# Attention and a gated MLP in one kernel: an opening of 108 tiny matmuls, queries loaded without their zeros, and a new order

## The chip, the cores and the metric

The kernel runs on one core of a Trainium2 chip. The metric is the device time of one execution in microseconds, the median of several runs; lower is better.

## The reference

`q`, `k`, `v` have 8 batches, 8 heads, 576 positions and 64 columns; `x` then has 4608 tokens of 512.

```python
scores = 1/sqrt(64) * q @ k.T
rel = pos[:, None] - pos[None, :]
mask_local = (rel >= 0) & (rel < 32)                       # heads 0 to 3
mask_strided = (rel >= 0) & (pos[None, :] % 32 == pos[:, None] % 32)   # heads 4 to 7
attn = softmax(where(mask, scores, -1e9))                  # the sum has 1e-9 added
x = (attn @ v), heads side by side                         # (4608, 512)
xn = x / sqrt(mean(x * x, -1) + 1e-6) * rms_g
g = xn @ w_gate                                            # 512 -> 1536
out = (g * sigmoid(g) * (xn @ w_val)) @ w_out              # 1536 -> 512
```

## The kernel before

**Attention.** A unit is one batch and one pair of heads; there are 32, numbered 0 to 31. For each unit TensorE computes the scores (`unit_s`; S0, S1, ... below) only where the mask can let something through: 576 queries of two heads lie on 128 partitions, and for each there are 9 groups of 64 keys. VectorE takes the maximum of each group of 64 (L726, L730), ScalarE the exponentials, in nine activations that also give the sums (L743), VectorE multiplies by the reciprocal (L766, L767, L775) and transposes 32x32 blocks (L776), and TensorE multiplies with the values (`unit_o`; P0, P1, ... below). Unit 3 is the one unit in `HALFQ`: there VectorE subtracts the maximum (L736), one activation takes the exponential of all 576 columns (L762), and VectorE sums (L763).

For units 0 to 7 (`EIGHT`) the queries of the two heads come from DRAM as one block of 128 x 1152 with zeros in it: in the 64 partitions of one head the columns of the other head are zero, so that one matmul with a stationary operand of 128 x 64 serves both heads. The mask is added on TensorE by two bf16 matmuls with the identity ahead of the scores (L706), and `scores` (L718) then issues 18 f32 matmuls; the trace shows 36, since the compiler splits each in two. The values take 40, shown as 80 (L810). Units 0 to 3 (`NPRO`) are the prologue: their inputs lie in slots of their own.

**MLP.** The tokens go in 9 chunks of 512. Chunk 0 is done plainly, while the weights are still being converted: `gemm1` gives gate (key g) and value (key v) for each of 12 blocks of 128 columns of d_ff, "d_ff unit 0 to 11", and `slot_o` adds to the output in the banks a0 to a3, which ScalarE empties at the end (L1164). Chunks 1 to 8 go in pairs with a scheme of seven products for eight (L1250 for gate and value, L1403 for the output). Every f32 operand is split into a high and a low part, and a product takes three matmuls. The weights are split and combined once, by VectorE and ScalarE, and spilled to DRAM (`gvd`, `od`, `wd`), from where the later chunks load them. The sum of squares of chunk 0 goes through a matmul with ones (L888).

**Order.** Nothing in the code's order of statements fixes what runs when. Each operation is handed to `op` with an estimated cost; `Plan.order` and `Plan.forward` then go through all operations by list scheduling with these costs and the table `DUE` (one priority for each operation) and write the program of each engine in that order. `PLACE` says which slot of SBUF each group of tiles uses. Where the plan has TensorE idle for more than `FILLA` ns in the first 50 us, `fill` puts matmuls there that multiply zeros (`still`, L616) into a bank that is written afresh later; they compute nothing. The program of each engine is in order, and an instruction waits for semaphores of the others. PSUM banks are named g, v, a0 to a3 and pair (two banks); in the rows that order the instructions a0 to a3 are a_85 to a_88, and bl_N is a tile in a slot.

**The opening.** The first operation on TensorE comes some time after the start, and `fill` puts ten wide fillers (512 columns) ahead of it. Pool sets `still` to zero (L612):

```python
    op("Pool", 100, 0, lambda: nc.gpsimd.memset(still, 0.0), writes=["still"])
    def fill(n, pad):
        for _ in range(n):
            nc.tensor.matmul(out=pad[:, CH - FILLN:CH], lhsT=still[:, 0:P], rhs=still[:, 0:FILLN], ...
```

The order on TensorE is then S0, S1, S2, a filler, P0, S3, P1, a filler, P2, three fillers with three gate matmuls of d_ff unit 0 among them, P3, two fillers, S4, three value matmuls, the sum of squares, nine gate matmuls, three value matmuls, S5, and on.

## Time and profile before

| | |
|---|---|
| time, median of 3 runs | 909.78 us (908.98 to 911.97) |
| profiled execution | 910.43 us, of which the span 908.7 |
| TensorE clock granted, mean | 0.994 of full |
| busy: TensorE matmul, weight load | 886.8 us (98%), 716.8 us |
| busy: VectorE, ScalarE, GpSimd | 713.1 us (78%), 544.7 us (60%), 1.2 us |
| DMA | 234.25 MB, 258 GB/s in the mean |

The busy shares are means over the whole span; the first 60 us, where the attention of the first units, the conversion of the weights and chunk 0 run side by side, are not like the rest. The rows below are of the profiled execution, in us from the start of its span.

### The profile page before, as it was taken

The numbers are of one execution on the slowest core, as the hardware profiler recorded it, in microseconds if no ns is written. First come the engines' busy times: TensorE is split into PE (matmuls) and PEld (weight loads), VectorE is DVE, ScalarE is ACT, GpSimd is POOL, SyncE is SP. The second block draws the span as 40 slices with busy tenths as digits, with TensorE's granted clock in tenths as the row PEclk, the third lists the DMA queues.
The fourth block names the chain that finished last, engine by engine and source line by source line (L and its number), as shares of the span: only waits on it lengthen the run. The fifth ranks groups of instructions, "written<-read, shape, count | busy, mean of one in ns | idle before, by whom it ended". The sixth has DMA issues, their size and how long they took to land.

```text
span 908.7 us, 20785 instructions
## 1 busy us (share of the span) xinstructions
PE 886.8 (98%) x8289; PEld 716.8 (79%) x8292; DVE 713.1 (78%) x1203; ACT 544.7 (60%) x1179; POOL 1.2 (0%) x12
## 2 busy tenths in 40 slices
PE   6899999899999999999999999999999999999998
PEld 4677778678878888888887888888888888888886
DVE  4889989999998999667679998554799973338982
ACT  6799978677777784455537673444559533333440
POOL 0000000000000000000000000000000000000000
PEclk9899999999999999999999999999999999999999
DMA  9799999989987857876747559955365796742741
GB/s 357 269 400 413 413 414 366 403 330 403 359 286 272 284 175 268 292 269 195 231 145 243 169 172 334 341 161 179 105 196 174 230 369 214 210 148 70 248 136 69
DMA packets 104512, 234.25 MB, mean 258 GB/s; under 512 B 11616, under 2 KB 13920, under 8 KB 102112
## 3 DMA queue, kind: packets, MB, share of 16 engines
q1 hardware_dynamic: 103696, 232.34, 73.2%
q8 instruction: 65, 1.06, 0.5%
q10 hardware_dynamic: 720, 0.59, 0.2%
q14 instruction: 31, 0.25, 0.1%
HBM read 180.98 MB, written 51.90 MB: 256 GB/s over the span
## 4 chain that ended last, share of the span: by engine, by line
PE 82%; DMA 10%; DVE 3%; ACT 3%; issue 1%; SPq 0%; DVEq 0%
PE a L1250 22%; PE g L1250 14%; PE v L1250 14%; PE a L1403 11%; PE g L1403 7%; PE v L1403 7%; DMA wd<-bl 3%; DMA gvd<-bl 2%; DMA od<-bl 2%; PE pair L712 2%; PE pair L797 1%; DMA bl<-in_kT_dram 1%; PE a L797 1%; ACT pp L743 1%; DMA xk<-in_kT_dram 1%
## 5 line engine op out<-in xcount | busy, mean ns | idle before, releaser
L1250 PE MATMUL a<-bl,bl 128*128 128x512 f32 x856 | 216.7, 394 | 3.9 <-ACT bl L1164 3.0
L1250 PEld LDWEIGHTS a<-bl,bl 128*128 128x128 f32 x856 | 158.2, 188 | 39.2 <-ACT bl L1164 3.8
L594 ACT CAST bl<-bl 128x512 fp32r<-128x512 f32 (+1 forms) x209 | 126.7, 638 | 80.3 <-DVE bl L1206 37.6
L602 DVE TENSOR_TENSOR bl<-bl,bl 128x512 fp32r<-128x512 f32 x244 | 159.9, 687 | 8.2 <-ACT bl L594 2.1
L1250 PE MATMUL v<-bl,bl 128*128 128x512 f32 x571 | 146.0, 390 | 0.0
L1250 PE MATMUL g<-bl,bl 128*128 128x512 f32 x567 | 145.1, 390 | 0.0
L1206 DVE TENSOR_TENSOR bl<-bl,bl 128x512 f32<-128x512 f32 x169 | 113.7, 687 | 35.1 <-ACT bl L1267 33.5
L1250 PEld LDWEIGHTS v<-bl,bl 128*128 128x128 f32 x571 | 106.8, 188 | 23.1 <-DVE bl L1288 0.6
L1250 PEld LDWEIGHTS g<-bl,bl 128*128 128x128 f32 x567 | 106.0, 188 | 23.1 <-DVE bl L1288 0.7
L1262 DVE TENSOR_TENSOR a<-a,bl 128x512 f32<-128x512 f32 x96 | 66.6, 697 | 72.6 <-PE a L1250 61.8
L1403 PE MATMUL a<-bl,bl 128*128 128x512 f32 x418 | 97.5, 390 | 0.0
L1403 PEld LDWEIGHTS a<-bl,bl 128*128 128x128 f32 x418 | 78.2, 188 | 16.5
L1403 PE MATMUL g<-bl,bl 128*128 128x512 f32 x269 | 65.4, 390 | 0.0
L1403 PE MATMUL v<-bl,bl 128*128 128x512 f32 x269 | 65.0, 389 | 0.0
L1258 ACT COPY bl<-g 128x512 f32<-128x512 f32 x48 | 28.2, 588 | 52.8 <-PE g L1250 49.2
L1267 ACT ACTIVATE bl<-a 128x512 f32<-128x512 f32 x48 | 28.7, 601 | 51.9 <-DVE a L1262 50.2
L1403 PEld LDWEIGHTS v<-bl,bl 128*128 128x128 f32 x269 | 50.5, 188 | 10.5
L1403 PEld LDWEIGHTS g<-bl,bl 128*128 128x128 f32 x269 | 50.3, 188 | 10.6
L1258 ACT COPY bl<-v 128x512 f32<-128x512 f32 x48 | 28.2, 587 | 43.4 <-PE v L1250 42.1
L973 DVE TENSOR_TENSOR bl<-bl,bl 128x512 fp32r<-128x512 f32 (+1 forms) x54 | 45.9, 859 | 0.2
L596 DVE CAST bl<-bl 128x512 fp32r<-128x512 f32 (+1 forms) x89 | 39.1, 452 | 7.2 <-PE v L1250 1.6
L1258 ACT COPY bl<-a 128x512 f32<-128x512 f32 x48 | 28.0, 587 | 22.6 <-PE a L1250 22.4
(163 smaller groups left out, 1159.1 us busy)
## 6 DMA issues: line engine op xcount, KB each, us to landing
bl<-gvd SPq DMA_DIRECT2D x288, 256.0 KB, 4.4
bl<-od SPq DMA_DIRECT2D x168, 256.0 KB, 3.5
gvd<-bl SPq DMA_DIRECT2D x12, 1024.0 KB, 8.2
bl<-in_wgv_dram SPq DMA_DIRECT2D x11, 1024.0 KB, 10.2
wd<-bl SPq DMA_DIRECT2D x18, 512.0 KB, 9.7
bl<-wd SPq DMA_DIRECT2D x18, 512.0 KB, 6.8
vt<-in_vl_dram SPq DMA_DIRECT2D x24, 352.0 KB, 6.1
xk<-in_kT_dram SPq DMA_DIRECT2D x28, 288.0 KB, 5.0
```

The source lines that it names most:

```text
L594: nc.scalar.copy(out=o, in_=i)
L596: nc.vector.tensor_copy(out=o, in_=i)
L602: elementwise(CH, lambda e: both(e).tensor_tensor(out=lo.new(F32R), in0=src(), in1=hi.f32(), op=ALU.subtract), reads + [hi.key], [lo.key])
L712: nc.tensor.matmul(out=pr[at // CH][32 * r:32 * r + 32, at % CH:at % CH + KW], lhsT=tq()[hd, q0:q0 + 32], rhs=tk_()[hd, q0:q0 + KW], start ...
L797: nc.tensor.matmul(out=ends[r % 2][0][n][64 * h:64 * h + 64, at + 32 * lo:at + 32 * hi], lhsT=va()[32 * r:32 * r + 32, D * (6 * n + j):D * ...
L973: elementwise(len(l) * 256, lambda e, l=l, zs=zs: both(e).tensor_tensor(out=sides(l, 1, F32R), in0=cols(zs), in1=sides(l, 0), op=ALU.subtr ...
L1206: elementwise(CH, lambda e: both(e).tensor_tensor(out=o.new() if fresh else o.t, in0=a.t, in1=b.t, op=how), [a.key, b.key], [o.key])
L1250: nc.tensor.matmul(out=banks[bk], lhsT=w, rhs=xs[k][y].t, start=start and k == 0 and i == 0, stop=stop and k == 1 and i == 2, skip_group_c ...
L1258: op("ACT", act(CH, True), 0, lambda: nc.scalar.copy(out=t.new(), in_=banks[bk]), reads=[bk], writes=[t.key])
L1262: op("DVE", dve(CH), 0, lambda: nc.vector.tensor_tensor(out=banks[bk], in0=banks[bk], in1=t.t, op=ALU.add), reads=[t.key], writes=[bk])
L1267: op("ACT", act(CH, True), 0, lambda: nc.scalar.activation(out=t.new(), in_=banks[bk], func=AF.Silu), reads=[bk], writes=[t.key], tab="silu")
L1403: nc.tensor.matmul(out=banks[bks[j]], lhsT=v, rhs=xs[k][y].t, start=start and k == 0 and i == 0, stop=stop and k == KT - 1 and i == 2, ski ...
```

## The change

**The opening.** `first` takes the place of the first call of `fill`: 108 matmuls with a stationary operand of 32 x 64 and 32 columns of zeros, in turn into the banks g, v, a0 and a1, and then 2 wide fillers (`FIRST = (108, 2)`) instead of 10. In the trace the compiler will again show two for each of the 108. `still` is set by VectorE, as its first operation, instead of by Pool.

**The queries of units 0 to 7** are loaded without their zeros: two DMAs of 64 partitions x 576 elements (144 KB each) instead of one of 576 KB. The zero halves are set on the chip, by VectorE for units 0 and 1 (`BLANK`), by Pool for units 2 to 5, which share their buffers with the later ones. The queries lie in another order, so that the stationary operand of a score's matmul takes 64 elements at a step of 18 (`NROW`), 72 bytes, instead of 64 in a row.

**Unit 3** is no longer in `HALFQ`: its exponentials are nine activations with sums, as those of the other units.

**Costs and order.** The planner's costs change (`SLOWS`, `SLOWV`, a term of the scores, `FILLS`), as do the banks into which fillers may go, and `PLACE` and `DUE` are new throughout, so that the order on every engine is new.

```diff
+BLANK = 2
-SLOWS = 700.0
-SLOWV = 700.0
+SLOWS = 0.0
+SLOWV = 100.0
-FILLS = 400.0
+FILLS = 300.0
+FIRST = (108, 2)
 PLACE = list(bytes.fromhex(
-    "080c18281c16242c2e003402513f303a4908120456054c4110220f46204e3d43361e5a45501826200c1422322a18100034080634181c12300e405324"
...
+    "00281026202c181614322e1e004b264a5d242a295c363c570624054c1151374d47524f504d202426101830322a0c043400081202201c062e220f5343"
...
-HALFQ = (3,)
+HALFQ = ()
...
             if e == "PE" and s < FILLZ:
-                if s - was > FILLA and self.pads[i]:
+                if not started:
+                    started = True
+                    out.append(lambda pad=self.pads[i]: self.first(pad))
+                elif s - was > FILLA and self.pads[i]:
...
+    still = sbt([P, max(256, FILLN)], "still", BF16)
+    op("DVE", 200, 0, lambda: nc.vector.memset(still, 0.0), writes=["still"], early=1e6)
...
-    op("Pool", 100, 0, lambda: nc.gpsimd.memset(still, 0.0), writes=["still"])
...
+    def first(pad):
+        z = still.bitcast(F32)
+        for i in range(FIRST[0]):
+            r, h = 32 * (i % 4), 64 * (i // 4 % 2)
+            nc.tensor.matmul(out=banks[("g", "v", "a0", "a1")[i % 4]][h:h + 64, 0:32], lhsT=z[r:r + 32, 0:64], rhs=z[r:r + 32, 0:32], start=True, stop=True, skip_group_check=True)
+        fill(FIRST[1], pad)
...
-            op("Pool", 100, 0, lambda: nc.gpsimd.memset(tk_()[:, 0:PAD], 0.0), writes=keys_[2:])
-        op("SP", 430, 0, lambda: nc.sync.dma_start(out=tq(), in_=qz[i] if i < EIGHT else qT[i - EIGHT]), writes=keys_[:1], bytes_=P * S * 4 * n, rel=REL.get(i, 0.0), follow="SP" if pro else None)
+            def blank(x):
+                x.memset(tk_()[:, 0:PAD], 0.0)
+                for h in range(2):
+                    x.memset(tq()[64 * h:64 * h + 64, S * (1 - h):S * (2 - h)], 0.0)
+            x = ("DVE", nc.vector) if i < BLANK else ("Pool", nc.gpsimd)
+            op(x[0], 750 if i < BLANK else 1300, 0, lambda: blank(x[1]), writes=keys_[2:])
+        for h in range(n):
+            op("SP", 430, 0, lambda h=h: nc.sync.dma_start(out=tq()[64 * h:64 * h + 64, S * h:S * h + S] if n > 1 else tq(), in_=qc[i, 64 * h:64 * h + 64] if n > 1 else qT[i - EIGHT]),
+               writes=[keys_[0] + (h,)], bytes_=P * S * 4 // n, run=2304, rel=REL.get(i, 0.0), follow="SP" if pro else None)
...
-                    nc.tensor.matmul(out=pr[at // CH][64 * s:64 * s + 64, at % CH:at % CH + KW], lhsT=tq()[:, 2 * q0:2 * q0 + 64], rhs=tk_()[:, q0:q0 + KW],
+                    nc.tensor.matmul(out=pr[at // CH][64 * s:64 * s + 64, at % CH:at % CH + KW], lhsT=tq().rearrange("p (m r) -> p m r", r=NROW)[:, :, NBL * s + n], rhs=tk_()[:, q0:q0 + KW],
...
-        op("PE", SCO[i >= EIGHT] + 500 * quick + (SLOWS if i in (4, 5) else 0), 0, scores, reads=kin + (["cb" + "1" * (p // 2), "identb"] if quick else []),
-           writes=keys_, pad=pr[1], soon=SOON[i >= EIGHT][0])
+        op("PE", SCO[i >= EIGHT] + 200 * quick + (SLOWS if i in (4, 5) else 0), 0, scores, reads=kin + ["still"] * (i == 0) + (["cb" + "1" * (p // 2), "identb"] if quick else []),
+           writes=keys_, pad=pr[1] if i < NPRO else banks["v"] if i == NPRO else None, soon=SOON[i >= EIGHT][0])
```

The lines behind `first` and `blank` move down by 18, so that L706 of before is L724 of after, L718 is L736, L973 is L991, L1164 is L1182.

**TensorE around S4.** In the order before, these rows stand between P2 and S5: three gate matmuls (L1106, bank g), then, behind P3, the last mask matmul of S4 and its scores (L718), and the value matmuls of d_ff unit 0 (L1096, bank v) and the sum of squares (L888) ahead of the rest of the gate's.

```order
L1106 MATMUL g<-bl_416,bl_469 128x512
L1106 MATMUL g<-bl_463,bl_469 128x512
L1106 MATMUL g<-bl_478,bl_469 128x512
...
L706 MATMUL pair<-cb,identb 128x256
L718 MATMUL pair<-xk_63,xq_65 64x64 x18
L1096 MATMUL v<-bl_416,bl_547 128x512 x2
...
L888 MATMUL a_86<-bl_406,ones 128x512
L1106 MATMUL g<-bl_545,bl_469 128x512
...
L1096 MATMUL v<-bl_463,bl_547 128x512 x2
...
L706 MATMUL pair<-cb,identb 128x256
L718 MATMUL pair<-xk_64,xq_66 64x64 x18
```

After, the same place reads as follows (L620 is a filler, L1124 the gate, L1114 the value, L906 the sum of squares).

```order
L724 MATMUL pair<-cb,identb 128x256
L736 MATMUL pair<-xk_63,xq_65 64x64 x18
L1124 MATMUL g<-bl_539,bl_651 128x512
L1124 MATMUL g<-bl_645,bl_651 128x512
...
L620 MATMUL a_85<-still 128x512
L1124 MATMUL g<-bl_709,bl_651 128x512
...
L1124 MATMUL g<-bl_663,bl_651 128x512
...
L736 MATMUL pair<-xk_64,xq_66 64x64 x18
L906 MATMUL a_86<-bl_301,ones 128x512
...
L620 MATMUL a_85<-still 128x512
...
L1114 MATMUL v<-bl_539,bl_651 128x512 x2
```

All twelve gate matmuls now stand behind S4, and all value matmuls behind S5, the sum of squares and six fillers. Ahead of S4 the order is now S0, S1, S2, two fillers, S3, one filler, P0, four fillers, P1, four fillers, P2, P3, three fillers.

**VectorE around S4's maximum.** Before, the low part of d_ff unit 0's weight, 2 x 256 columns to a half (L973 subtracts the high part, L596 makes that), is finished ahead of the maximum of S4 (L726).

```order
L935 SCALAR_TENSOR_TENSOR bl_542<-bl_351,few,bl_416 128x512
L596 CAST bl_547<-bl_197 128x2x256
L880 TENSOR_TENSOR bl_136<-bl_535 128x512
L973 TENSOR_TENSOR bl_547<-bl_197,bl_547 128x2x256
L935 SCALAR_TENSOR_TENSOR bl_574<-bl_535,few,bl_545 128x512
L884 TENSOR_TENSOR bl_406<-bl_406,bl_136 128x512
L726 TENSOR_REDUCE st_76<-pair 128x9
L730 TENSOR_SCALAR st_76<-st_76 128x9
```

After, from the maximum of S4 (now the first L744; the second is S5's) to the second half of that weight's low part (L991, into bl_651, which all matmuls of d_ff unit 0 read). Lines left out are small ones of 9 columns.

```order
L744 TENSOR_REDUCE st_76<-pair 128x9
...
L953 SCALAR_TENSOR_TENSOR bl_709<-bl_472,few,bl_692 128x512
L902 TENSOR_TENSOR bl_301<-bl_301,bl_694 128x512
L898 TENSOR_TENSOR bl_726<-bl_647 128x512
L902 TENSOR_TENSOR bl_301<-bl_301,bl_132 128x512
L601 CAST bl_651<-bl_595 128x2x256
L902 TENSOR_TENSOR bl_301<-bl_301,bl_726 128x512
...
L1029 SCALAR_TENSOR_TENSOR bl_132<-bl_167 128x1024
L793 TENSOR_TENSOR pp_69<-pp_69,st_76 128x576
L744 TENSOR_REDUCE st_77<-pair 128x9
...
L794 STREAM_TRANSPOSE pT_71<-pp_69 128x576
L991 TENSOR_TENSOR bl_651<-bl_595,bl_651 128x2x256
```

The second half of the weight's low part has moved from ahead of S4's maximum to 15 places behind it.

**ScalarE at the end of chunk 0.** The rows with what each instruction waits for (DMAHW is a lane of the DMA queues); before, the emptying of a0 to a3 is spread over seven places, and its first waits for a DMA, VectorE and TensorE.

```order
L1258 COPY bl_2119<-v 128x512 [waits DMAHW0_49,PE_49]
L1164 ACTIVATE bl_140<-a_85,few 128x512 [waits DMAHW2_49,DVE_49,PE_49]
L594 CAST bl_574<-bl_159 128x512 [waits DVE_49]
L594 CAST bl_2101<-bl_2093 128x512 [waits DVE_49]
L1164 ACTIVATE bl_2119<-a_87,few 128x512 [waits PE_49]
L1164 ACTIVATE bl_1200<-a_86,few 128x512 [waits Activation_49]
L594 CAST bl_2101<-bl_744 128x512 [waits DVE_49]
L1164 ACTIVATE bl_140<-a_88,few 128x512 [waits PE_49]
```

After, the four stand together, the first waits for TensorE alone and the second also for a DMA.

```order
L599 CAST bl_2261<-bl_2022 128x512 [waits DVE_49]
L1182 ACTIVATE bl_932<-a_85,few 128x512 [waits PE_49]
L1182 ACTIVATE bl_658<-a_86,few 128x512 [waits DMAHW7_49,PE_49]
L1182 ACTIVATE bl_661<-a_87,few 128x512 [waits PE_49]
L1182 ACTIVATE bl_661<-a_88,few 128x512 [waits PE_49]
```

No cast stands between them any more.

## Rows read from the trace of the kernel before

**Rows 1.** The page: span; part 1, busy time and instructions; part 3, instruction queue.

```profile
span 908.7 us, 20785 instructions
...
PE 886.8 (98%) x8289; PEld 716.8 (79%) x8292; DVE 713.1 (78%) x1203; ACT 544.7 (60%) x1179; POOL 1.2 (0%) x12
...
q8 instruction: 65, 1.06, 0.5%
```

**Rows 2.** Table by stage: busy us (instructions begun) per engine, granted clock, DMA share, GB/s.

```profile
0.00:5.90 5.90, 3.79 (x11) 1.26 (x11) 0.27 (x4) 1.52 (x3) 1.06 (x11) 1.00 0.70 232
0.00:18.00 18.00, 11.25 (x220) 7.08 (x221) 8.19 (x26) 11.10 (x59) 1.24 (x12) 1.00 0.92 344
18.08:24.40 6.32, 4.64 (x127) 3.98 (x127) 4.79 (x11) 4.47 (x10) 0.00 (x0) 0.73 1.04 403
24.40:30.53 6.13, 4.92 (x126) 3.45 (x127) 5.83 (x11) 2.65 (x7) 0.00 (x0) 0.72 0.83 331
100.00:160.00 60.00, 60.00 (x577) 48.42 (x576) 54.92 (x94) 49.75 (x106) 0.00 (x0) 1.00 1.00 395
```

**Rows 3.** TensorE's timeline: start, us, what, count, idle before it and what ended that.

```profile
6.24 0.80 PE L718 MATMUL g<-bl 128*64 128x64 f32 x20
...
8.84 1.27 PE L718 MATMUL a<-bl 128*64 128x64 f32 x36 [0.97 <-DMA bl<-in_kT_dram]
...
11.94 1.27 PE L718 MATMUL a<-bl 128*64 128x64 f32 x36 [1.27 <-DMA bl<-in_kT_dram]
...
18.09 1.42 PE L718 MATMUL pair<-bl 128*64 128x64 f32 x23 [2.33 <-issue]
19.44 2.40 PE L810 MATMUL a<-pT,bl 32*64 32x64 f32 x80
...
24.41 1.31 PE L810 MATMUL a<-bl,bl 32*64 32x64 f32 x57 [1.26 <-issue]
...
30.54 0.46 PE L810 MATMUL pair<-bl,bl 32*64 32x64 f32 x16 [1.00 <-issue]
...
33.66 2.01 PE L718 MATMUL pair<-xk,xq 128*64 128x64 f32 x36
...
42.40 4.25 PE L1096 MATMUL a<-bl,bl 128*128 128x512 f32 x18
...
48.85 1.39 PE L810 MATMUL pair<-pT,vt 32*64 32x64 f32 x80 [1.52 <-ACT pp L743]
...
56.97 2.34 PE L1096 MATMUL v<-bl,bl 128*128 128x512 f32 x9 [0.41 <-DVE bl L1133]
```

**Rows 4.** Table by stage, the stretch behind the second hole.

```profile
25.00:28.50 3.50, 3.28 (x45) 1.95 (x41) 3.20 (x6) 2.38 (x6) 0.00 (x0) 0.51 1.04 416
```

**Rows 5.** Timeline of the first 6 us: setting `still`, and the wide fillers.

```profile
1.06 0.52 POOL L612 MEMSET still<- 128x512 bf16 x1
...
1.64 3.79 PE L616 MATMUL v<-still 128*128 128x512 bf16 x10 [1.64 <-POOL still L612]
```

**Rows 6.** Groups of VectorE's instructions from 5 to 52 us: busy us, mean ns.

```profile
L973 DVE TENSOR_TENSOR bl<-bl,bl 128x512 fp32r<-128x512 f32 x6 | 3.9, 684 | 0.0
...
L776 DVE STREAM_TRANSPOSE pT<-pp 128x576 f32<-128x576 f32 x3 | 2.3, 777 | 0.1
L726 DVE TENSOR_REDUCE st<-pair 128x9 f32<-128x576 f32 x3 | 2.2, 747 | 3.1 <-PE pair L718 3.1
```

**Rows 7.** Groups of ScalarE's instructions, shapes apart, 5 to 52 us.

```profile
L743 ACT ACTIVATE pp<-pair,st 128x64 f32<-128x64 f32 x18 | 5.4, 327 | 0.7 <-DVE st L730 0.7
```

**Rows 8.** Timeline of all engines near 165 us.

```profile
164.36 1.22 DVE L973 TENSOR_TENSOR bl<-bl,bl 128x1024 fp32r<-128x1024 f32 x1
...
165.66 0.69 ACT L1164 ACTIVATE bl<-a,few 128x512 f32<-128x512 f32 x1 [1.29 <-issue]
...
166.41 1.67 PE L1250 MATMUL a<-bl,bl 128*128 128x512 f32 x6 [2.38 <-ACT bl L1164]
```

**Rows 9.** The page, part 5: costliest groups; the number behind the bar: idle before them.

```profile
L1250 PE MATMUL a<-bl,bl 128*128 128x512 f32 x856 | 216.7, 394 | 3.9 <-ACT bl L1164 3.0
```

More of the change, by code (lines that the diff above doesn't have):

```diff
@@ L348, in order @@
         self.lengths.append(max(t[3] for t in took))
-        out, was = [], 400.0
+        out, was, started = [], 400.0, False
         for i, e, s, _ in took:
             if e == "PE" and s < FILLZ:
-                if s - was > FILLA and self.pads[i]:
+                if not started:
+                    started = True
+                    out.append(lambda pad=self.pads[i]: self.first(pad))
+                elif s - was > FILLA and self.pads[i]:
                     out.append(lambda n=int((s - was - FILLB) / FILLS), pad=self.pads[i]: self.fill(n, pad))
@@ L616, in fill @@
             nc.tensor.matmul(out=pad[:, CH - FILLN:CH], lhsT=still[:, 0:P], rhs=still[:, 0:FILLN], start=True, stop=True, skip_group_check=True)
-    plan.fill = fill
+    def first(pad):
[4 more added lines that the diff above has]
+        fill(FIRST[1], pad)
+    plan.fill, plan.first = fill, first
     units = [(b, p) for b in range(NB) for p in range(NH // 2)]
@@ L1602, in tr @@
         return np.ascontiguousarray(by_residue(a).reshape(NB, NH // 2, 2, S, D).transpose(0, 1, 2, 4, 3)).reshape(NB, NH // 2, P, S)
-    def apart(a, h, n):
-        z = np.zeros(a.shape[:-1] + (2, n), a.dtype)
-        z[..., 0, :] = np.where(h == 0, a, 0)
-        z[..., 1, :] = np.where(h == 1, a, 0)
-        return z
     part = np.arange(P)
@@ L1614, in _layout @@
     vz = np.ascontiguousarray(vp[:, :, (part // 32 % 2)[:, None], idx]).reshape(-1, P, (NBL + 1) * D)[:EIGHT]
-    qz = apart(tr(q).reshape(NB, NH // 2, P, NROW, 32), (part // D)[:, None, None], 32).reshape(-1, P, 2 * S)[:EIGHT]
     head = part[:, None] // 64 ^ (np.arange(NVB) >= 6)[None, :]
```

295 lines of the change are left out of this document (148 added, 147 removed).

## The prediction

> **What bounds the kernel now.** I read the page's busy times first, then the table by stage, then TensorE's waits. The span is 908.7 us and TensorE is busy for 886.8 of it, far more than VectorE or ScalarE [rows 1]. From 100 to 160 us it is busy for all 60.00, although the DMA engines are then full too (share 1.00, 395 GB/s) [rows 2]. So the end is a sum of TensorE's work and its holes, and no edit to a load or a side engine counts unless it closes a hole or cuts TensorE's instructions. The holes lie mostly in the first 60 us, with one place near 165 us.
>
> The timeline of TensorE shows what the early holes are [rows 3]. S0 starts at 6.24. Three holes lie inside a burst of small matmuls whose inputs had all arrived: at 18.09, 24.41 and 30.54 the rest of S3, of P2 and of P3 starts after 2.33, 1.26 and 1.00 us put down to "issue", together 4.6. Up to the first of them TensorE has begun 220 matmuls, between the first and the second 127, between the second and the third 126 [rows 2], whatever the burst. The page has 65 transfers of instructions on queue q8 and 8289 + 8292 TensorE instructions [rows 1], which is 255 for each transfer, or about 127 matmuls with their loads. So I read the holes as waits for the next block of instructions, wanted at matmul 221, 348 and 474. The work goes on at 18.09, 24.41 and 30.54, 6.3 and 6.1 us apart: in a burst a block takes 6.2 us. Matmul 94, one block before 221, is near the start of S2, at about 12.0 (86 stand ahead of it and its two mask matmuls; S2's scores start at 11.94), and the block wanted at 221 is there 6.1 us later. So crossing a border seems to call the block after next, and that takes about 6.1 us.
>
> After each hole the clock is low: granted 0.51 of full in 25 to 28.5 us [rows 4], which is 1.2 instead of 2.4 GHz, and 0.73 and 0.72 in the mean of the two stretches between the holes [rows 2]. P1 takes 2.40 us there, P4 1.39 at full clock; S4 takes 2.01, S1 1.27 [rows 3].
>
> The Trainium skill ("Runtime: NRT & Kernel Launch", Instruction fetch mechanics) also has instructions come in blocks of 256, and says that crossing a border is "mostly hidden". The 255 in each transfer agrees with it; the three holes do not. By its word, the tiny matmuls would win nothing and the first term below would have only its loss.
>
> **The tiny matmuls.** The 108 are split in two by the compiler, as the scores are (36 in a score's row of the timeline for 18 in the program). So 216 tiny and 2 wide ones, 218 in all, stand before S0. With S0 to S3 and P0 to P3 as ordered (38 and 80 matmuls) and the fillers between, the borders fall thus: 94 inside the tiny ones, 221 at the first matmul of S0's scores, 348 in S3, 475 in P1, 602 in P2, 729 in S4 with 13 matmuls to go.
>
> When is the block at 221 there? No row shows a tiny matmul. The nearest are P1 and P4, 80 matmuls in 2.40 and 1.39 us: 30 and 17 ns each. The ten wide fillers of before took 3.79 us [rows 5], 0.38 each against 0.24 for the same shape later (18 gemm matmuls in 4.25 [rows 3]), so the start is slow too. They began at 1.64, when Pool had set `still` (1.06 + 0.52 [rows 5]); VectorE now does that first, so I take a start near 1.2. Then 94 tiny ones end between 2.8 and 4.0; I take 3.4. The call then takes at most the 6.1 us above, seen with DMA shares near 1.04, and at least nothing that S0 feels. Before 5.9 us the share is 0.70 [rows 2], so I scale: 0.70 x 6.1 = 4.3, an estimate, and S0 goes on at 7.7. Bounds: 6.2, S0's start today, and 10.1 (the latest 4.0 with 6.1).
>
> From there a block takes 6.2 us while the burst lasts: 13.9, 20.1, 26.3, 32.5. S4 ends 0.5 later, at 33.0; it ended at 35.67 before (33.66 + 2.01) [rows 3]. That is 2.7 us gained, with bounds 4.2 and 0.3.
>
> **What is late next.** Two debts stand against it. First, three gemm matmuls ran before S4 and now run behind: 3 x 0.236 = 0.7 us. Second, the value gemm of d_ff unit 0 needs the second half of its weight's low part, and VectorE makes that only 16 instructions after it has S4's scores. From 24.40 to 30.53 it was busy 5.83 us for 11 instructions [rows 2], 0.53 each, overlaps taken off; 16 take 8.5. By kinds: ten of 512 or 576 columns at 0.68 to 0.78 (7.2) [rows 6], one of 1024 at 1.22 [rows 8], a cast and four small ones, 9.5 less overlaps, so the 8.5 stands and the gemm starts at 41.5. TensorE has 12 gate matmuls (2.8), S5 with its masks (1.7) and the sum of squares (0.5) for that time, so it is free at 38.0 and waits 3.5 us, part of it filled by six fillers that do nothing. Before, the same work waited 1.52 at P4 and 0.41 at the value gemm [rows 3], so this costs 1.6 us. Opening: -2.7 + 0.7 + 1.6 = -0.4 us, between -1.9 and +2.0.
>
> **Queries, zeros, exponentials.** Eight units load 288 KB less each, 2.3 MB or 5.9 us of DMA at 395 GB/s. S1 and S2 waited 0.97 and 1.27 us for keys [rows 3], but with S0 held to 7.7 those waits are covered, and from 100 to 160 us TensorE has no hole to give; I take 0. The zeros are 64x576 fills on VectorE and Pool: VectorE has done 0.27 us of work by 5.9 us, Pool 1.06 [rows 2], and Pool's 512-column fill takes 0.52 us [rows 5], so they fit ahead of the data. Unit 3 now takes nine activations with sums on ScalarE, 2.7 us at 18 in 5.4 [rows 7], where it had one of 576 columns, and saves VectorE two passes like the reduction of [rows 6], 1.5 us. ScalarE is idle for 5.3 us between 18.08 and 30.53 [rows 2] to hide it. The queries are read as stationary operand at a step of 72 bytes; no row shows such a load. Taken as 0, with the rival below as upper bound.
>
> **The hole near 165 us.** TensorE waits 2.38 us for ScalarE to empty bank a0 of chunk 0's output (L1164) [rows 8], and all waits of that matmul group on bank a come to 3.9 [rows 9]. ScalarE itself stands still for 1.29 us ahead of that; the instruction waits for VectorE as well as TensorE (see the order), and starts at 165.66, when VectorE's L973 (164.36 + 1.22) has ended [rows 8]: its destination was still being read. In the new order that instruction waits for TensorE alone and the four stand together. I take the 2.4 as gone and the others as they are; bounds 0 and 3.9.
>
> **Sum.** -0.4 - 2.4 = -2.8 us. The profiled execution took 910.43 us for its 908.7 us span, 0.65 over the median of 909.78. So 910.43 - 2.8 = 907.6 there, and 907.0 against the median.
>
> **Rivals.** (B) The block at 221 is there in time: the opening gives 1.9, and with the whole 3.9 near 165 us closed, 910.43 - 1.9 - 3.9 = 904.6, less 0.65: 904.0. For it: the light DMA load before 5.9 us. Against: 6.1 us in the one chain that I could follow. (C) It changes nothing: the stalls only move to S0 and to the value gemm (opening +1 to +2), and the bank's emptying gains all or little, since the second of the four now waits for a DMA. From 909.8 + 1.4 - 2.4 to 909.8 + 0.5, so 908.8 to 910.3. (D) Slower: a stationary load at a 72-byte step. 36 pairs of load and matmul take 1.27 us, 35 ns each; if the load doubles this, a score takes 1.27 us more. S0 to S3 hide in part behind the blocks, S4 to S7 do not: 4 x 1.27 + 1 = 6.1, so 907.0 + 6.1 = 913.1. It turns the sign from a factor of about 1.5 and passes 0.3% from 1.9. For it: nothing in the trace, but nothing against it either, since no load of before has a step.
>
> **Numbers.** This forecast 0.42, between 904.5 and 909: 0.28 of it faster by over 0.3% (below 907.05, about what this measurement tells from no change), 0.14 within. B 0.23, faster. C 0.18, within. D 0.17, slower. So faster 0.51, same 0.32, slower 0.17. The range reaches 1.5 below B, for debts that turn out hidden too, takes in C whole, and stops 0.6 short of D's price: 902.5 to 912.5.
>
> **What would show it.** Right: an "issue" hole inside S0 that ends near 7.7 and none at the old places; S4 ending near 33; fillers and then a wait for VectorE ahead of the value gemm, near 41.5; no wait for the bank's emptying at chunk 0's end. Wrong: score matmuls longer than 35 ns each at full clock; S0 on time; S4 ending after 35; a new wait between 60 and 180 us, where slots were placed anew.

## The result, and the profile after

The changed kernel took 915.86 us in the median of ten runs (913.03 to 919.67), the kernel before, run beside it, 910.38 (908.98 to 912.82). The ratio is 1.0061, with an interval from 1.0042 to 1.0081: slower by 0.6%, or 5.5 us, where 907.0 was forecast. The profiled execution took 919.49 us, one of the two longest of the ten, so its last microseconds are not typical; the split by causes below rests on medians.

The page after: span, TensorE's busy time and instructions (part 1), the instruction queue (part 3), and the group that empties bank a0 (part 5).

```profile
span 917.7 us, 21294 instructions
...
PE 898.5 (98%) x8513; PEld 728.2 (79%) x8513; DVE 725.3 (79%) x1240; ACT 538.4 (59%) x1166; POOL 5.2 (1%) x17
...
q8 instruction: 67, 1.10, 0.5%
...
L1268 PE MATMUL a<-bl,bl 128*128 128x512 f32 x857 | 216.4, 394 | 1.3 <-ACT bl L1182 1.3
```

Against [rows 1] TensorE's idle time fell, from 21.9 us (908.7 - 886.8) to 19.2, and its busy time rose by 11.7. So the change closed holes, as meant, and made the work itself longer by more. All waits of the group that writes bank a behind chunk 0 are down from 3.9 us [rows 9] to 1.3.

The table by stage, the first 18 us after (columns as in [rows 2]):

```profile
0.00:18.00 18.00, 14.71 (x368) 12.41 (x370) 7.79 (x24) 8.92 (x52) 5.03 (x16) 0.91 0.92 264
```

The DMA engines are as busy as in the same stretch of [rows 2], share 0.92, but move 264 GB/s where they moved 344.

TensorE's timeline after (columns as in [rows 3]):

```profile
7.27 0.30 PE L724 MATMUL g<-cb,identb 128*128 128x320 bf16 x1 [2.09 <-DMA cb<-in_consts_dram]
7.61 1.51 PE L736 MATMUL g<-bl 128*64 128x64 f32 x20
...
16.16 2.30 PE L736 MATMUL pair<-bl 128*64 128x64 f32 x36
...
24.62 1.15 PE L828 MATMUL a<-bl,bl 32*64 32x64 f32 x61 [0.56 <-DVE bl L794]
29.59 0.79 PE L828 MATMUL a<-bl,bl 32*64 32x64 f32 x18 [3.82 <-issue]
...
34.45 1.60 PE L736 MATMUL pair<-xk,xq 128*64 128x64 f32 x23
36.62 1.02 PE L736 MATMUL pair<-xk,xq 128*64 128x64 f32 x13 [0.57 <-issue]
...
46.20 3.10 PE L1114 MATMUL v<-bl,bl 128*128 128x512 f32 x12
...
54.63 2.31 PE L736 MATMUL pair<-xk,xq 128*64 128x64 f32 x36
...
124.46 6.55 PE L1169 MATMUL a<-bl,bl 128*128 128x512 f32 x21 [1.80 <-issue]
...
174.77 5.73 PE L1268 MATMUL a<-bl,bl 128*128 128x512 f32 x24 [1.33 <-ACT bl L1182]
```

In the kernel before, the first row that needs the mask constants is this one:

```profile
5.89 0.31 PE L706 MATMUL g<-cb,identb 128*128 128x320 bf16 x1 [0.46 <-DMA identb<-in_consts_dram]
```

Four things stand in these rows. S0 waits until 7.27 for the mask constants, which were there at 5.89 in the kernel before. Each score (36 pairs of load and matmul) takes 2.30 us, 64 ns a pair, also at full clock (S3 at 16.16, with 1.00 granted from 16.0 to 18.5 us), where S1 took 1.27 [rows 3]. The holes put down to "issue" are at the two places that the count of blocks gave, in P2 and in S4 with 13 matmuls left, but the one in P2 lasts 3.82 us, and S4 ends at 37.64 where it ended at 35.67. And there is a new one of 1.80 us at 124.46; the 21 matmuls behind it take 6.55 us at a granted clock of 0.75 (first row below, of the table by stage), and the same 21 take 5.10 in the version with ten wide matmuls in place of the tiny ones (e5_wide, second row, of its timeline):

```profile
124.40:131.00 6.60, 6.54 (x22) 5.31 (x23) 4.09 (x16) 4.84 (x16) 0.00 (x0) 0.75 1.03 418
...
120.09 5.10 PE L1169 MATMUL a<-bl,bl 128*128 128x512 f32 x21
```

What the "issue" holes wait for can be read from the trace's records of the instruction queue q8, which give the start and the length of each transfer. In the changed kernel one transfer ends at 28.20 us and P2 goes on at 29.59; one ends at 35.18 and S4 goes on at 36.62; one ends at 123.12 and the work goes on at 124.46. In the traces of all twenty kernels there are 61 holes of 0.45 us or more put down to "issue", and each ends 1.2 to 1.7 us after a transfer on q8 has ended. So they are waits for blocks of instructions, as the prediction read them.

### The profile page after: what moved, and what is told of

The parts are those of the page before. It is cut to its first block, busy times and chain, and to the rows that moved or that the text cites. A ratio compares the mean times of both kernels' runs of the same rounds, so it can differ in the third digit from the quotient of the medians.

```text
span 917.7 us, 21294 instructions
## 1 busy us (share of the span) xinstructions
PE 898.5 (98%) x8513; PEld 728.2 (79%) x8513; DVE 725.3 (79%) x1240; ACT 538.4 (59%) x1166; POOL 5.2 (1%) x17
## 4 chain that ended last, share of the span: by engine, by line
PE 90%; DMA 4%; DVE 2%; issue 1%; ACT 1%; SPq 0%; ACTq 0%; DVEq 0%
PE a L1268 21%; PE g L1268 14%; PE v L1268 14%; PE a L1421 11%; PE g L1421 7%; PE v L1421 7%; PE v L1114 3%; PE g L1114 3%; PE a L1169 3%; PE pair L730 2%; PE pair L815 2%; DMA bl<-in_kT_dram 2%; PE pair L736 1%; PE a L815 1%; DMA xq<-in_qc_dram 1%
## 5 line engine op out<-in xcount | busy, mean ns | idle before, releaser
L1224 DVE TENSOR_TENSOR bl<-bl,bl 128x512 f32<-128x512 f32 x171 | 115.7, 688 | 41.6 <-ACT bl L1285 39.7
L1268 PE MATMUL g<-bl,bl 128*128 128x512 f32 x570 | 146.3, 391 | 0.6 <-DVE bl L601 0.3
L1268 PE MATMUL v<-bl,bl 128*128 128x512 f32 x568 | 145.5, 391 | 0.0
L1268 PEld LDWEIGHTS g<-bl,bl 128*128 128x128 f32 x570 | 106.5, 188 | 24.6 <-DVE bl L1306 1.4
L1268 PEld LDWEIGHTS v<-bl,bl 128*128 128x128 f32 x568 | 106.2, 188 | 23.2 <-DVE bl L1306 0.4
L1421 PE MATMUL g<-bl,bl 128*128 128x512 f32 x286 | 68.1, 390 | 0.0
L1421 PE MATMUL v<-bl,bl 128*128 128x512 f32 x286 | 67.8, 389 | 0.0
L1421 PEld LDWEIGHTS v<-bl,bl 128*128 128x128 f32 x286 | 53.7, 188 | 11.1
L1421 PEld LDWEIGHTS g<-bl,bl 128*128 128x128 f32 x286 | 53.5, 188 | 11.3
L991 DVE TENSOR_TENSOR bl<-bl,bl 128x512 fp32r<-128x512 f32 (+1 forms) x54 | 45.8, 861 | 0.2
```

Of the source, the lines that this page charges most:

```text
L991: elementwise(len(l) * 256, lambda e, l=l, zs=zs: both(e).tensor_tensor(out=sides(l, 1, F32R), in0=cols(zs), in1=sides(l, 0), op=ALU.subtr ...
L1224: elementwise(CH, lambda e: both(e).tensor_tensor(out=o.new() if fresh else o.t, in0=a.t, in1=b.t, op=how), [a.key, b.key], [o.key])
L1268: nc.tensor.matmul(out=banks[bk], lhsT=w, rhs=xs[k][y].t, start=start and k == 0 and i == 0, stop=stop and k == 1 and i == 2, skip_group_c ...
L1421: nc.tensor.matmul(out=banks[bks[j]], lhsT=v, rhs=xs[k][y].t, start=start and k == 0 and i == 0, stop=stop and k == KT - 1 and i == 2, ski ...
```

## The experiments

The change has four parts that can be had apart: the new order (with unit 3's activations), the 72-byte step of the stationary operand, the queries' loads without zeros, and the 108 tiny matmuls. The theory after the result was that step, loads and tiny matmuls each cost time and the order wins some; the rivals were that one part carries the whole loss, or that the order does. Medians stand beside ratios to the kernel before, run on the same chip, with their 95% intervals in brackets.

### The order alone, and with single parts

**e9_order**: the new order, with the queries' loads and layout of before and ten wide opening matmuls.

```diff
-FIRST = (108, 2)
+FIRST = (0, 10)
...
-lhsT=tq().rearrange("p (m r) -> p m r", r=NROW)[:, :, NBL * s + n]
+lhsT=tq()[:, 2 * q0:2 * q0 + 64]
...
-nc.sync.dma_start(out=tq()[64 * h:64 * h + 64, S * h:S * h + S], in_=qc[i, 64 * h:64 * h + 64])
+h or nc.sync.dma_start(out=tq(), in_=qc[i])
```

> The new order, new costs and unit 3's nine activations alone: the kernel after with one load of 128 x 1152 with zeros for each of units 0 to 7, no step, and the ten wide fillers of before. What is left of the change here is the order. Theory A (the order itself is good, what spoils it are the half loads, the tiny matmuls and the step): 906 to 909.5, with no 2.4 us hole near 165 us. Theory B (the order is worse): 911 or more.

907.89 us, 0.9974 [0.9965, 0.9982]: 2.4 us faster than before, the fastest version of all. Its table by stage, and rows of TensorE's timeline:

```profile
0.00:18.00 18.00, 12.50 (x241) 7.87 (x245) 7.51 (x25) 10.86 (x64) 0.50 (x8) 1.00 0.92 343
```

```profile
29.41 0.80 PE L826 MATMUL pair<-bl,bl 32*64 32x64 f32 x18 [2.74 <-issue]
...
32.01 2.19 PE L734 MATMUL pair<-xk,xq 128*64 128x64 f32 x36
...
42.98 2.79 PE L1112 MATMUL v<-bl,bl 128*128 128x512 f32 x11 [0.67 <-DVE bl L989]
...
165.09 5.74 PE L1266 MATMUL a<-bl,bl 128*128 128x512 f32 x24 [1.33 <-ACT bl L1180]
```

The loads move 343 GB/s again, and the wait for a0 is the 1.33 us of the changed kernel: that gain is the order's. The value gemm does wait for VectorE, 0.67 us.

**e14_order_step** adds the 72-byte step to it, **e10_order_first** the tiny matmuls; **e5_wide** is the changed kernel with ten wide matmuls for the tiny ones.

> The new order with full loads, ten wide fillers and the step of 72 bytes in the stationary operand. The step took 1.03 us more for each of 8 scores and 2 us of time in the order of before. Theory (S0 to S3 hide it behind loads and blocks, S4 to S7 do not): 909 to 911.5; what is missing from there to the 913.0 of after with ten wide fillers is then the price of the half loads. Rival (the step is most of the 5 us between these two): 912 to 913.

> The new order with full loads and no step (907.9 by itself) and the 108 tiny matmuls. Theory (the opening costs by where the borders fall): 910 to 913. Rival (this order suits them): 908.5 or less.

> The kernel after with the opening of before: ten wide fillers and no tiny matmul; loads, step and order as after. In the order of before the tiny matmuls alone cost 4.7 us (914.9 against 910.2). Theory 1 (they cost here too, since they move the borders of the instruction blocks into P1 and P2, where a hole of 3.82 us stands in the trace of after): 910 to 912. Rival (here S0 waits for its mask constants until 7.27 anyway, which covers the first block, so the tiny matmuls cost nothing or help): 915 to 919, with new holes put down to issue inside P0 and P1.

911.40 us, 1.0017 [1.0008, 1.0026]; 911.99, 1.0021 [1.0008, 1.0033]; 913.04, 1.0028 [1.0017, 1.0039], the last between its two expectations. In a chain of ratios times 910: order -2.4; with the step +1.5, so the step costs 3.9; with compact loads +2.5, another 1.0, which is within the intervals; with the tiny matmuls +5.6, another 3.0. On the order without the step the tiny ones cost 4.3, on the old order 5.1 (e4_first, below): a part's price depends on what else is there. In the new order no part carries the whole.

The hole near 124 us belongs to the tiny matmuls. It is in e10_order_first too, whose profiled execution took 912.19 us, near its median (first row below, of TensorE's waits: engine, what, releaser, us, times, longest), and not in e5_wide. And with the changed kernel's own loads, but wide matmuls, the constants are there at 6.13 (e5_wide's timeline):

```profile
PE a L1167 <- issue: 1.4, 1, 1.4
...
6.13 0.40 PE L724 MATMUL g<-cb,identb 128*128 128x320 bf16 x1 [0.49 <-DMA cb<-in_consts_dram]
```

So of the 1.4 us by which S0's constants came later than in the kernel before, 0.2 comes with the loads and the order, and 1.1 with the tiny matmuls. In the changed kernel the first instruction transfer on q8 runs from 4.61 to 5.77 us, ahead of the constants' landing; that it held them up is argued from its length of 1.16 us and not tested.

### The step

**e1_stride**: the kernel before, with the queries laid out so that the stationary operand has the 72-byte step and nothing else changes.

```diff
-lhsT=tq()[:, 2 * q0:2 * q0 + 64]
+lhsT=tq().rearrange("p (m r) -> p m r", r=NROW)[:, :, NBL * s + n]
```

> The kernel before with one edit: the queries of units 0 to 7 lie in another order, so that the stationary operand of a score's matmul takes its 64 elements at a step of 72 bytes; loads, zeros and order as before. Theory 1 (the step is what costs): the trace of after has 2.30 us for a score's 36 matmuls, 64 ns a pair, where before has 1.27 and 35; so S0 to S7 take 1.03 us more each, 8.2 in all, of which S0 to S3 may hide up to half behind late instruction blocks: 4 to 8 us slower, 914.5 to 918.5. Theory 2 (the new order and the opening cost, and the step hides): 2.30 us in the trace as well, but under 2 us slower.

912.12 us, 1.0023 [1.0014, 1.0032]. TensorE's timeline shows why 1 us for a score does not add up over eight scores:

```profile
18.04 1.61 PE L718 MATMUL pair<-bl 128*64 128x64 f32 x23 [0.87 <-issue]
...
33.54 2.36 PE L718 MATMUL pair<-xk,xq 128*64 128x64 f32 x36
...
49.70 1.39 PE L810 MATMUL pair<-pT,vt 32*64 32x64 f32 x80
```

S3's rest starts at 18.04, as in [rows 3], after 0.87 us of waiting where it was 2.33: the longer scores used up the wait for the block. S4, which runs behind the holes while the clock is low, takes 2.36 where it took 2.01 [rows 3], 0.35 more and not 1. P4 no longer waits (1.52 in [rows 3]). So 2.1 us are left of the loss.

**e3_steps**: one step for each of units 4 to 7 of the kernel before: 8, 12, 24 and 36 bytes.

```diff
+STEP = (1, 1, 1, 1, 2, 3, 6, 9)
...
-lhsT=tq()[:, 2 * q0:2 * q0 + 64]
+lhsT=tq().rearrange("p (o m r) -> p o m r", m=64, r=STEP[i])[:, (NBL * s + n) // STEP[i], :, (NBL * s + n) % STEP[i]]
```

> The kernel before with steps of 8, 12, 24 and 36 bytes in the stationary operand of the scores of units 4, 5, 6 and 7, units 0 to 3 as before. It prices the step: if any step costs the same, S4 to S7 take 64 ns a pair each (2.3 us at full clock); if the cost grows with the step, it lies between 35 and 64 ns, in this order; if only a step past some size costs, the small ones stay at 35 ns (1.27 us).

A single execution, 911.09 us. TensorE's timeline, S4 to S7:

```profile
32.74 1.30 PE L719 MATMUL pair<-xk,xq 128*64 128x64 f32 x36
...
38.89 1.81 PE L719 MATMUL pair<-xk,xq 128*64 128x64 f32 x36
...
50.38 2.29 PE L719 MATMUL pair<-xk,xq 128*64 128x64 f32 x36
...
62.31 2.39 PE L719 MATMUL pair<-xk,xq 128*64 128x64 f32 x36
```

36, 50, 64 and 66 ns a pair: 8 bytes are free, 12 are not, and from 24 on nothing more is lost. The Trainium skill ("SBUF — State Buffer", Specifications (TRN2)) says that SBUF is read in lines of 16 bytes and that fewer than two reads to a line cost bandwidth. These rows agree: two fp32 elements fall in a line at 8 bytes, one or two at 12, one from 16 on.

**e6_step2**: the changed kernel with a step of 8 bytes. The compact half then lies in runs of 256 bytes instead of one long one.

```diff
+STEP = 2
...
-x.memset(tq()[64 * h:64 * h + 64, S * (1 - h):S * (2 - h)], 0.0)
+x.memset(tq()[64 * h:64 * h + 64].rearrange("p (o h x) -> p o h x", h=2, x=32 * STEP)[:, :, 1 - h], 0.0)
...
```

> The kernel after with its queries in groups of 2 blocks, so that the stationary operand's step is 8 bytes instead of 72 and the loads write runs of 256 bytes; nothing else. With a step of 8 bytes unit 4 took 36 ns a pair, as without a step. Theory 1 (what the step costs lies on the path behind S4): S4 to S7 1.03 us shorter each, 3 to 6 us under after, 910 to 913. Theory 2 (the step hides, as most of it did in the order of before, where it cost 2 us of 8): 1 to 2.5 us under after, 913.4 to 915. If short runs slow the loads, S0 to S3 start later and it is no faster than after.

914.72 us, 1.0048 [1.0033, 1.0062]: hardly better than the changed kernel. In the first 20 us the loads move 237 GB/s, in the changed kernel 274. TensorE's timeline has the fast scores, and what took their gain:

```profile
8.15 0.30 PE L725 MATMUL g<-cb,identb 128*128 128x320 bf16 x1 [2.74 <-DMA cb<-in_consts_dram]
...
18.08 1.31 PE L737 MATMUL pair<-bl 128*64 128x64 f32 x36 [1.63 <-DMA bl<-in_kT_dram]
```

The constants come at 8.15 instead of 7.27, and the keys are late for S3. The step's cost is removed, the loads' is larger. The edit also shortens the runs, so it does not price the step alone.

### The loads

**e11_halves**: the kernel before, the same bytes, but each load of queries split into two of 64 partitions.

```diff
-nc.sync.dma_start(out=tq(), in_=qz[i])
+for h in range(2):
+    nc.sync.dma_start(out=tq()[64 * h:64 * h + 64], in_=qz[i, 64 * h:64 * h + 64])
```

> The kernel before with the same bytes, but each load of queries split in two, partitions 0 to 63 and 64 to 127. In after the DMA engines moved 274 GB/s in the first 20 us at a share of 0.94, where before moved 350 at 0.93. Theory 1 (a transfer that covers 64 partitions moves at about half the rate, so halving the bytes in this way gains nothing): below 300 GB/s in the first 20 us at the same share, S1 to S3 wait longer, 3 to 10 us slower. Rival (the lower rate of after comes from its smaller transfers or its order): 340 GB/s or more, and the time within 1 us of before.

922.34 us, 1.0133 [1.0112, 1.0154]: 12 us lost by the split alone, more than the 3 to 10 expected. Its table by stage:

```profile
0.00:18.00 18.00, 12.97 (x179) 7.97 (x182) 5.75 (x20) 7.62 (x41) 1.06 (x11) 1.00 0.93 218
```

The busy share does not show it (0.93, before 0.92); the rate does, 218 GB/s against 344 [rows 2]. The Trainium skill ("SBUF — State Buffer", section "Door 1: The DMA port swizzle (why `[64,N]` ≈ `[32,N]`)") says that 64 neighbouring partitions reach only half of the 16 ports by which DMA enters SBUF. The 218 GB/s agree with a limit of that kind. No run separates it from a cost of the second transfer as such.

**e2_full**: the changed kernel with the zeros loaded, in two transfers of 64 partitions, and no step.

```diff
-x.memset(tq()[64 * h:64 * h + 64, S * (1 - h):S * (2 - h)], 0.0)
...
-nc.sync.dma_start(out=tq()[64 * h:64 * h + 64, S * h:S * h + S], in_=qc[i, 64 * h:64 * h + 64])
+nc.sync.dma_start(out=tq()[64 * h:64 * h + 64], in_=qc[i, 64 * h:64 * h + 64])
```

> The kernel after with its queries loaded with their zeros again (two DMAs of 64 partitions x 1152) and the stationary operand contiguous; order, tiny matmuls and unit 3 as after. Theory 1 (the step costs): a score takes 1.27 us again, and the time is 4 to 8 us below that of after, 908 to 912. Theory 2 (order and opening cost): within 2 us of after, 914 to 918. If the zeros left out were worth something, S0 to S3 wait longer for DMA here than in after.

923.77 us, 1.0143 [1.0130, 1.0156]. It was meant to restore the loads of before and did not, which led to e11_halves. Against e10_order_first (1.0021), which differs in whole loads alone, the split costs 11 us here. TensorE's timeline:

```profile
9.49 0.42 PE L722 MATMUL g<-cb,identb 128*128 128x320 bf16 x1 [4.06 <-DMA cb<-in_consts_dram]
```

**e7_compact** and **e8_compact2**: the kernel before with compact halves and the zeros set on chip, at steps of 72 and 8 bytes (the second differs in `STEP = 2` for `STEP = 18`).

```diff
-nc.sync.dma_start(out=tq(), in_=qz[i])
+for h in range(2):
+    nc.sync.dma_start(out=tq()[64 * h:64 * h + 64].rearrange("p (o h x) -> p o h x", h=2, x=32 * STEP)[:, :, h], in_=qz[i, 64 * h:64 * h + 64].rearrange("p (o x) -> p o x", x=32 * STEP))
```

> The kernel before with the compact queries alone: two loads of 64 x 576 for one of 128 x 1152, zeros set by VectorE (units 0, 1) and GpSimd, VectorE sets the zeros of the fillers, step of 72 bytes; opening, order and unit 3 as before. To be held against the same kernel with the step alone (912.1). Theory 1 (fewer bytes pay: S1 and S2 no longer wait 0.97 and 1.27 us for DMA): 909 to 911.5. Rival (the 2.3 MB were hidden behind late instruction blocks, and two issues in place of one put the mask constants behind them): S0 starts up to 1.4 us later, 912 to 914.

> The kernel before with the compact queries and a step of 8 bytes (runs of 256 bytes in the load), the rest as in the run with the step of 72 bytes. Theory 1: 2 us under that run, and if fewer bytes pay, under before: 907.5 to 909.5. Rival: within 1 us of before.

913.81 us, 1.0039 [1.0024, 1.0054], and 913.73, 1.0032 [1.0017, 1.0046]. Neither beats e1_stride or the kernel before: half the bytes of the queries, moved at a lower rate (276 GB/s over the first 18 us in e7_compact, 344 before), win nothing. The 8-byte step wins nothing either, against the expectation: TensorE's waits for "issue" are 2.6 us twice in e8_compact2, where e7_compact has 1.5, 1.0 and 0.8.

**e12_queues**: the changed kernel, with the second half of units 0 to 3 sent from ScalarE's queue, so that both halves could be under way together.

```diff
-nc.sync.dma_start(
+(nc.scalar if h and pro else nc.sync).dma_start(
```

> The kernel after with the second half of the queries of units 0 to 3 issued from ScalarE's queue, so that both halves are under way together; the rest as after. Theory 1 (one half at a time uses half of the paths into SBUF): with both at once the rate of the first 9 us rises from 256 GB/s towards 350, the mask constants are there before 7.27, and the time falls by 1 to 4 us. Rival (the rate per transfer is not what S0 to S3 wait for): within 1 us of after.

915.70 us, 1.0062 [1.0045, 1.0079]: no help. The constants come later still, in TensorE's timeline:

```profile
8.71 0.45 PE L724 MATMUL g<-cb,identb 128*128 128x320 bf16 x1 [3.29 <-DMA cb<-in_consts_dram]
```

The trace's records of transfers show packets of both queues side by side: from 6 to 9 us the two moved 0.53 MB together, where the changed kernel's one queue moved 0.78. So a second queue did not bring the rate back. Which halves met is not recorded, and this neither supports nor excludes the limit by ports.

### The tiny matmuls

**e4_first**: the kernel before with the 108 tiny and two wide matmuls. **e13_first77**, **e15_first72**, **e16_first88**: the same with 77, 72 and 88.

```diff
+FIRST = (108, 2)
...
+for i in range(FIRST[0]):
+    r, h = 32 * (i % 4), 64 * (i // 4 % 2)
+    nc.tensor.matmul(out=banks[("g", "v", "a0", "a1")[i % 4]][h:h + 64, 0:32], lhsT=z[r:r + 32, 0:64], rhs=z[r:r + 32, 0:32], start=True, stop=True, skip_group_check=True)
+fill(FIRST[1], pad)
```

> The kernel before with the opening alone: 108 tiny matmuls and 2 wide fillers in place of 10 wide fillers; order, loads and unit 3 as before, GpSimd still sets the zeros. Theory 1 (the opening moves the borders of the instruction blocks, and its block comes while TensorE waits for its first data): the holes leave matmul 221, 348 and 474 of the old count, and the time falls by 0.3 to 4 us. Rival (the holes only move): holes of the same sum at other places, the time within 1 us of before.

914.87 us, 1.0056 [1.004, 1.0072]. TensorE's timeline:

```profile
8.84 0.74 PE L729 MATMUL g<-bl 128*64 128x64 f32 x17 [2.11 <-issue]
...
22.09 1.04 PE L821 MATMUL a<-pT,bl 32*64 32x64 f32 x56 [2.75 <-issue]
...
28.45 0.58 PE L821 MATMUL a<-bl,bl 32*64 32x64 f32 x9 [2.88 <-issue]
```

S0's scores stop at once and go on at 8.84, inside the bounds given (6.2 to 10.1) and 1.1 behind the 7.7 taken. But the holes do not get fewer: 2.11 + 2.75 + 2.88 = 7.7 us, where before had 4.6 [rows 3]. In the changed kernel S0 has no such hole: the transfer on q8 ends at 5.77, and the constants come later than the block.

If only the places of the borders count, fewer tiny matmuls should put them where TensorE waits anyway.

> The kernel before with 77 tiny matmuls and 2 wide fillers, 156 in the trace, in place of 10 wide ones. By the count of blocks (a border every 127 matmuls, first wait at matmul 221, each block 6.1 us after the border before it was crossed) the borders then stand at the end of S1, behind the first matmuls of S3, in P2 where it starts on VectorE's word anyway, and in the second half of P3. Theory 1 (it is the place of the borders that counts): no hole in S1 and P2, about 1 us at S3, under 1 us in P3, and a time of 907.5 to 910, against 914.9 with 108. Rival (any such opening costs): 912 to 916.

909.90 us, 1.0002 [0.999, 1.0014]. TensorE's timeline:

```profile
15.91 0.33 PE L821 MATMUL v<-pT,bl 32*64 32x64 f32 x3 [0.26 <-issue]
...
22.20 2.39 PE L821 MATMUL a<-bl,bl 32*64 32x64 f32 x75 [0.54 <-issue]
...
75.69 0.74 PE L1107 MATMUL v<-bl,bl 128*128 128x512 f32 x2 [1.09 <-issue]
```

The early holes are nearly gone, and at 63 us this kernel is 3.2 us ahead of before. It loses 1.4 of that near 75 us and 1.2 near 226, where holes of about 1 us stand, and at the end 0.4 is left. So later borders move as well. From that came a count for them: harmless at 72, harmful at 88.

> The kernel before with 72 tiny matmuls and 2 wide fillers, 146 in the trace. With 77 the work was 3.2 us ahead of before at 63 us and lost 1.4 of it near 73 to 79 us and 1.2 near 226 to 233, in late bursts with a hole put down to issue. Theory (a border of the instruction blocks stands every 127 matmuls; two of them closer than 6.1 us make a hole; the count ahead sets where they stand, to the end of the program): taking the starts of the matmuls of before and shifting the borders by 136 gives no late hole over 0.6 us, so the early 3 us stay: 906.5 to 908.5. Rival (the late losses have nothing to do with the count): as with 77, 909 to 911.

> The kernel before with 88 tiny matmuls and 2 wide fillers, 178 in the trace. Theory (as for 72): the same shift gives holes of 2.9 us near 73 to 76 us and of about 3 us near 94 to 97, and with the low clock behind each, the time is 911 to 915, worse than with 72 or 77 although the early part gains as much. Rival (only the number of tiny matmuls costs, smoothly, 909.9 with 77 and 914.9 with 108): 911 to 912, without holes near 75 and 96 us.

909.48 us, 0.9998 [0.9986, 1.0009], and 916.63, 1.0071 [1.0053, 1.0089]. With 72 no late hole came, as expected, but two early ones did (TensorE's waits: engine, what, releaser, us, times, longest), and the 906.5 to 908.5 us expected were missed:

```profile
PE a L821 <- issue: 1.7, 1, 1.7
PE pair L729 <- issue: 1.5, 1, 1.5
```

With 88 two late holes came near the places that the count named: one ends at 76.57 (73 to 76 given), one at 102.20 (94 to 97 given). The time is above the 911 to 915 expected. TensorE's timeline:

```profile
76.57 0.41 PE L723 MATMUL pair<-xk,xq 64*32 64x64 f32 x18 [1.70 <-issue]
...
78.82 4.11 PE L1107 MATMUL g<-bl,bl 128*128 128x512 f32 x12
...
102.20 0.45 PE L723 MATMUL pair<-xk,xq 64*32 64x64 f32 x11 [3.14 <-issue]
```

The 12 gate matmuls behind the first take 4.11 us; the same 12 take 2.9 at full clock.

**e17_later36** adds 36 tiny matmuls ahead of P4 to the 77, to move the later borders to a count taken as harmless; **e18_later_only** has these 36 alone, which should give the harmful count without any change at the start.

```diff
+if i == 4:
+    for j in range(36):
+        r, h = 0, 64 * (j % 2)
+        nc.tensor.matmul(out=banks["a1"][h:h + 64, 0:32], lhsT=z[r:r + 32, 0:64], rhs=z[r:r + 32, 0:32], start=True, stop=True, skip_group_check=True)
```

> The kernel before with 77 tiny matmuls and 2 wide fillers ahead of S0, and 36 more tiny ones (72 in the trace) ahead of P4, where TensorE waits 1.45 us for ScalarE anyway. Theory (the count ahead places the borders, up to the end): the opening keeps its 3.2 us, as with 77 alone, and behind P4 the borders stand 72 matmuls earlier, where the starts of the run with 77 give no hole over 0.6 us; so the 3 us stay, 906 to 908, the first version of the old order clearly faster than before. Rival (the late losses come back elsewhere, or the tiny ones cost as much as they give): 909 to 911.

> The control: the kernel before with its ten wide fillers, and the 36 tiny matmuls ahead of P4 alone. Theory: up to P4 all is as before (1.52 us of waiting there hides most of them); behind it the borders stand 72 matmuls earlier, and the starts of before then give holes of 1.0 us near 76 and 3.1 us near 97 us, with the low clock behind: 912 to 916. Rival (what counts is the opening, not the count): 909.5 to 911, no new hole near 97 us.

908.66 us, 0.9988 [0.9976, 1.0000], and 910.74, 1.0005 [0.9994, 1.0017]. The first is at most a hair better than before and misses the 906 to 908 expected (its profiled execution took 914.76 us, far over its median, so its late rows are not read). The second refutes the count as a whole: the holes expected near 76 and 97 us did not come. These are all its waits of TensorE for "issue" of half a microsecond or more, all before 35 us:

```profile
PE a L827 <- issue: 1.9, 1, 1.9
PE pair L730 <- issue: 1.6, 1, 1.6
PE pair L827 <- issue: 0.8, 1, 0.8
```

By the records of q8 no transfer runs between 69.40 and 77.83 us there, around the scores where the first hole was expected; in e16_first88 one starts at 74.09, and the hole at 76.57 ends 1.5 us after its end. So the holes do come from the blocks; it is the count of matmuls that does not say when a block is fetched.

## Why the prediction was wrong, step by step

The forecast was -2.8 us, the medians give +5.5. Its terms, and what the chain of runs gives for each:

| term | forecast | measured | from |
|---|---|---|---|
| tiny matmuls, S4's end | -2.7 | +3.0 | changed kernel against e5_wide |
| debts behind S4 | +2.3 | +0.2 | rest of e9_order's -2.4 without the bank |
| bank a0 near 165 us | -2.4 | -2.6 | 3.9 [rows 9] to 1.3 |
| step of the stationary load | 0 | +3.9 | e14_order_step against e9_order |
| loads without zeros | 0 | +1.0 | e5_wide against e14_order_step |
| sum | -2.8 | +5.5 | |

The second row is a remainder, and the third is read from waits; no run has either alone.

**The tiny matmuls** are the largest error, 5.7 us. The step that failed is "From there a block takes 6.2 us while the burst lasts". The places of the borders were right to within a matmul (P2 after 61 of 80, S4 with 13 to go), their times were not. For P2's the working gave 26.3: it comes at 28.45 in e4_first and at 29.59 in the changed kernel, and S4's border, given as 32.5, at 36.62.

Two things were wrong in that step. First, the blocks did not set the pace from S0 to S3. From the border in S0 to the next, 127 matmuls on, TensorE itself took 7.3 us in e4_first (8.84 to 16.15), 0.75 of it a wait for VectorE, and 9.2 in the changed kernel (7.61 to 16.79). The clock behind S0's wait was low (0.61 granted from 8.8 to 13.2 us in e4_first, 0.67 from 7.3 to 10.0 in the changed kernel), and in the changed kernel each score was longer by the step. Second, a block takes longer in a loaded stretch: from one border to the next it took 6.4 us in e4_first (22.09 to 28.45), and in the changed kernel 7.6 (21.99 to 29.59) and 7.0 (29.59 to 36.62). So the chain was 2 to 4 us late, and the holes grew from 4.6 to 7.7 us (e4_first).

The low clock behind a hole stood in the text [rows 4], but in no term. The text also priced the borders only up to S4. One of the later ones fell into the attention matmuls near 124 us: 1.80 us, and 1.45 more behind it at the lower clock. The "mostly hidden" of the Trainium skill ("Runtime: NRT & Kernel Launch", Instruction fetch mechanics) disagrees with these holes too (0.57 to 3.82 us in the changed kernel).

**The step** was "Taken as 0, with the rival below as upper bound". No row spoke for 0, and rival D's mechanism is what happened, at a factor of 1.8 instead of 2. Its price was 6.1; 2.1 is left in the old order and 3.9 in the new, because some of the longer scores only use up waits, and at low clock a score is long without the step (2.19 us for S4 in e9_order). The sign of the forecast hung on it, as D said ("from a factor of about 1.5").

**The loads** were "I take 0", by the argument that covered transfers give nothing back. The bytes did halve, but the two transfers of 64 partitions that replace each one were not priced at all: the rate fell from 344 to 264 GB/s at the same share. What that cost in time, 1.0 us, is within the intervals. S0 "on at 7.7" came true (7.61), but by luck: the sign named was an "issue" hole inside S0, and S0 waited for its constants; in e4_first, where the hole is, it ends at 8.84.

**The hole near 165 us** was given as "the 2.4 as gone and the others as they are", and the size came out (-2.6), partly by luck. The four activations of ScalarE do stand together, at 174.04 us, but the hole named is not gone: TensorE still waits 1.33 us for ScalarE there, where it waited 2.38 [rows 8]. What made up the size is the two others of the kernel before, which were to stay and are gone:

```profile
168.69 3.26 PE L1250 MATMUL a<-bl,bl 128*128 128x512 f32 x13 [0.61 <-ACT bl L1164]
...
172.84 1.43 PE L1250 MATMUL a<-bl,bl 128*128 128x512 f32 x5 [0.90 <-DVE bl L973]
```

**The debts** were too large: the value gemm's wait for VectorE is there in e9_order, at 42.98 (41.5 given), but only 0.67 us long for 3.5, since six fillers and a later S4 cover the rest. In the changed kernel all is so late that it does not wait (46.20).

**Right**: TensorE as the bound (idle time fell while the time rose), the "issue" holes as waits for blocks of instructions, and the places of the first borders.

**Still open**: what decides whether a border in the later part makes a hole. e13_first77 and e16_first88 agreed with a count of matmuls in the main, e18_later_only did not. That TensorE's sequencer gets ahead within long gemm stretches and asks for blocks earlier there would explain it. The kernel before agrees in one place: behind the border at matmul 602, inside a gemm stretch, the transfer on q8 starts 0.24 us after that matmul (45.81), behind the four borders ahead of it, in bursts, 2.8 to 4.0 us after. No run tests it.

## What to carry to other kernels

Price a changed access pattern of a matmul's stationary operand, and a transfer cut to half of the partitions, with one small run before building an order on them: here the step, 64 against 35 ns a pair, by itself took more than the order had won, and whole loads cut in two (218 against 344 GB/s) cost 12 us. Moving the block borders of an instruction stream moves every later one too, so a gain at the start is not a gain until the rest of the trace has been read. When several edits come together, keep the one that pays: the order alone is 0.26% faster than before, and everything added to it here made it slower.
